# Two VectorE additions of a complex product, placed behind all 18 matmuls instead of behind the first six

## The chip, the cores and the metric

The kernel runs on one core of a Trainium2 chip. The metric is device time in microseconds (us) of one execution. Five engines work side by side, each through its own queue in order: TensorE (PE in the profile; its weight loads are PEld), VectorE (DVE), ScalarE (ACT), GpSimd (POOL) and SyncE (SP). [...] In this kernel SP issues most DMAs and POOL most loads of tables.

## The reference, cut to what matters

The first part of the computation takes a real Fourier transform along the 3072 positions of each of four sequences, multiplies the complex result by a complex 256 x 256 matrix, adds a complex bias, shrinks each part towards zero by 0.01, and transforms back:

```
X  = rfft(x, axis=1)                    # x: 4 x 3072 x 256
Yr = Xr @ w_r - Xi @ w_i + b_r
Yi = Xr @ w_i + Xi @ w_r + b_i
Y  = sign(Y) * max(|Y| - 0.01, 0)       # real and imaginary part apart
y  = irfft(Yr + 1j * Yi)
```

Two feed-forward blocks follow, the first with a gate (width 1024), the second of width 2048. All matrix products of the parts concerned here are made from a high and a low part of each operand: the product of a pair takes three matmuls (high by high, low by high, high by low).

## The kernel before, in words

The transform of length 3072 is split as 96 x 32. For each of the four sequences (called batches here, `b` = 0 to 3) there are three stages: `s1` (L292) transforms over 96 and writes to HBM, `mid` (L327) does the rest of the forward transform, the complex product, the shrinking and the first half of the way back, and `ib` (L442) the last transform, into HBM again. The change lies in `mid`.

`mid` makes 12 rounds, `j` = 0 to 11 (the loop at L407). One round consists of two steps, with a `yield` after each. In the first step come: `ia` (L391), which is the backward transform of an earlier round; the last part of the product before (the shrinking's second half at L379 on VectorE and four small DMAs `yz<-yf` at L382 on SP, which reorder the result); and `s2` (L332), which is eight matmuls, a ScalarE copy `Xh` (L159) and a VectorE subtraction `Xl` (L160) that make the high and the low part. In the second step, batches 1 to 3 first do `split_y` (L386), that is ScalarE's `yh` (L159), which waits for the four DMAs, and VectorE's `yl` (L160); `ia` of the next round's first step reads both. Then comes `mix` (L349).

`mix` makes the complex product with three real products. One PSUM tile `p` of 1024 columns (two banks) holds it: the common product `k1` in columns 512 to 767, that is in the second bank, and the two others in columns 0 to 511, the first bank. On PE it is six matmuls for `k1` and then twelve more (18 more in the first round of a batch). On VectorE there are two additions of `k1` and the bias into `y` (L368), and one addition of columns 0 to 511 to `y` (L375). Then ScalarE computes a `Relu` into `ym` (L377), and VectorE shrinks (L379).

The order of every queue is the order of the Python text, written out by hand (`manual_schedule` at L243): PE, ACT, DVE and POOL keep it. The framework adds the semaphore waits that the reads and writes of tiles call for. PSUM tiles of `s2`, `mix`, `ia`, and of the feed-forward's products share three buffers in turn (`ptile`, L154).

Batch 0 runs its rounds with little beside them but decoding of weights. The steps of batches 1 to 3 are fed one at a time (`feed`, L931) between the blocks of the first feed-forward part: each block is 12 matmuls with 512 columns on PE (`u_k`, L576: tile `pk`; `u_v`, L602: tile `acc`; `u_r`, L563: tile `pr`), with ScalarE and VectorE work for `g`, `gh` and `gl` (L588 to L597). So there is one such block between two steps, in most cases. Whether VectorE's `g` and `gl` stand between the product's additions and its shrinking, or not, depends on which of the two steps comes first in a unit of the feed-forward part; with nine steps to five units this turns over about every fifth round.

Of the kernel before, what the change touches and what calls it, by code (L numbers as in the profile page):

```python
# [107 lines left out]
def fourier_mix_ffn_kernel(  # L108
# [20 lines left out]
    nc = tc.nc  # L129
# [19 lines left out]
    def pad(pool, n):  # L149

        pads.append(n)
        pool.tile([128, n // 4], F32, name=f"pad{len(pads)}")

    def ptile(name):  # L154
        return ps.tile([128, 1024], F32, tag="h", name=name)

    def split(src, h, l):

        nc.scalar.activation(h, src, AF.Copy)  # L159
        nc.vector.tensor_sub(l, src, h.bitcast(F32))  # L160

    def three(o, pairs, first=True, last=True, **kw):

        n = 3 * len(pairs)
        i = 0
        for (lh, ll), (rh, rl) in pairs:
            for a, c in ((lh, rh), (ll, rh), (lh, rl)):
                nc.tensor.matmul(o, a, c, start=first and i == 0, stop=last and i == n - 1, **kw)  # L168
                i += 1
# [73 lines left out]
    with tc.manual_schedule(engines=order):  # L243
# [36 lines left out]
        def take(n):  # L280

            u = head["use"]
            load_chunks(u + n)
            r = [live.pop(u + i) for i in range(n)]
            head["use"] = u + n
            return r

        def fetch(n=AHEAD):

            load_chunks(head["use"] + n)  # L290
# [22 lines left out]
        def load_t(b, j):  # L313

            k = BEHIND[b]
            if j >= NP + k:
                b, j = b + 1, j - NP - k
            if b < B:
                if pad_t:
                    pad(fp, pad_t.pop())  # L320
                t = fp.tile([128, 2, 448], F32R if b else F32, tag="t", bufs=3, name="tt")
                c = slice(0 if j < NP else 192, 192 if j < BEHIND[b] else 448 if b else 320)
                eng = nc.gpsimd if b or j > 2 else nc.scalar
                eng.dma_start(out=t[:, :, c], in_=(tab if b else tab0)[j, :, :, c])
                tt[b, j] = t

        def mid(b):  # L327
            gb = sc_b[b].rearrange("(j g c) n d -> j (c n) g d", g=2, c=4)
            xx, yy = {}, {}
            behind = BEHIND[b]  # L330

            def s2(j):  # L332
                (a,) = take(1)
                t = tt[b, j].bitcast(F32) if b else tt[b, j]
                p = ptile("s2").rearrange("p (dt k g f) -> p dt k g f", dt=2, k=4, g=2)
                for g in range(2):
                    for dt in range(2):
                        w = a[:, g, 128 * dt : 128 * dt + 128]
                        m = 3 if j or g else 2
                        nc.tensor.matmul(p[:, dt, 0:m, g], w, t[:, g, 0 : 64 * m], start=True, stop=True)  # L340
                        if not (j or g):
                            nc.tensor.matmul(p[:, dt, 2:4, g], w, tex, start=True, stop=True)
                xh = fp.tile([128, 2, 448], F32R, tag="Xh", bufs=2, name="Xh")
                xl = fp.tile([128, 2, 448], F32R, tag="Xl", bufs=2, name="Xl")
                w = 384 if j else 448
                split(p.rearrange("p dt k g f -> p dt (k g f)")[:, :, 0:w], xh[:, :, 0:w], xl[:, :, 0:w])
                xx[j] = (xh, xl)

            def mix(j):  # L349
                xh, xl = xx.pop(j)  # L350
                p = ptile("mix")
                k1 = p[:, 512:768]
                part = lambda k, n=128: [
                    ((xh[:, dt, 128 * k : 128 * k + n], xl[:, dt, 128 * k : 128 * k + n]), dt) for dt in range(2)
                ]
                by = lambda w, xs: [(x, (w[0][:, dt], w[1][:, dt])) for x, dt in xs]
                three(k1, by(aw[0], part(2)))
                if pad_y:
                    pad(fp, pad_y.pop())
                y = fp.tile([128, 2, D], F32, tag="y", bufs=2, name="yf")  # L360
                m = fp.tile([128, 2, D], F32, tag="co", bufs=1, name="ym")
                z = fp.tile([128, 2, D], F32, tag="z", bufs=2, name="yz")
                if b:
                    yh = fp.tile([128, 512], F32R, tag="yh", bufs=2, name="yh")
                    yl = fp.tile([128, 512], F32R, tag="yl", bufs=2, name="yl")
                bs = bias[:, 0:2] if j else bias[:, 0::2]
                for a in range(2):
                    nc.vector.tensor_add(y[:, a], k1, bs[:, a])  # L368
                three(p[:, 0:256], by(aw[2], part(1)))
                pi = by(aw[1], part(0))  # L370
                three(p[:, 256:512], pi[:1], last=False)
                if j == 0:
                    three(p[0:64, 256:512], by(aw[0], part(3, 64)), first=False, last=False)
                three(p[:, 256:512], pi[1:], first=False)
                nc.vector.tensor_add(y, y, p[:, 0:512].rearrange("p (a e) -> p a e", a=2))  # L375
                yield
                nc.scalar.activation(m, y, AF.Relu, bias=lam2, scale=-1.0)  # L377
                yield
                nc.vector.scalar_tensor_tensor(y, m, -1.0, y, op0=ALU.mult, op1=ALU.max)  # L379
                for g in range(2):  # L380
                    for a in range(2):
                        nc.sync.dma_start(out=z[64 * a : 64 * a + 64, g], in_=y[64 * g : 64 * g + 64, a])  # L382
                z = z.rearrange("p g e -> p (g e)")
                yy[j] = (z, yh, yl) if b else z

            def split_y(j):  # L386
                if b:
                    y, *yy[j] = yy[j]
                    split(y, *yy[j])

            def ia(j):  # L391
                y = yy.pop(j)
                t = tt.pop((b, j + behind))[:, :, 192:448]
                p = ptile("ia") if b else pa.tile([128, 512], F32, tag="acc", name="ia0")
                for g in range(2):
                    c = slice(256 * g, 256 * g + 256)
                    if not b:
                        nc.tensor.matmul(p[:, c], t[:, g, 0:128], y[:, c], start=True, stop=True)
                        continue
                    yh, yl = y  # L400
                    three(p[:, c], [((t[:, g, 0:128], t[:, g, 128:256]), (yh[:, c], yl[:, c]))])
                sb = fp.tile([128, 2, D], F32, tag="ia", bufs=2, name="iasb")
                nc.scalar.activation(sb.rearrange("p g d -> p (g d)"), p[:, 0:512], AF.Copy)
                nc.sync.dma_start(out=gb[j], in_=sb)

            rest = iter(())
            for j in range(NP + 1):  # L407
                next(rest, None)
                if j < NP:
                    s2(j)  # L410
                if b or j:
                    load_t(b, j + 2)
                if j < NP:
                    yield
                    if j >= 2:
                        split_y(j - 2)
                if j:
                    rest = mix(j - 1)
                    next(rest)
                    fetch(AHEAD if b or j > 6 else 6)  # L420
                    next(rest)
                    yield
                if behind <= j < NP:
                    ia(j - behind)
            next(rest, None)
            split_y(NP - 2)

            def end(j):
                if j == NP - 1:
                    ready.add(("b", b))  # L430
                ia(j)
                if not b and j < NP - 1:
                    load_t(b, j + 6)

            if b:
                ends.extend([lambda: end(NP - 2), lambda: (load_t(b, NP + 3), split_y(NP - 1)), lambda: end(NP - 1)])
            else:
                ends.extend([lambda: end(NP - 3), lambda: end(NP - 2), lambda: end(NP - 1)])
# [670 lines left out]
```

## Time and profile before

| what | value |
|---|---|
| median of 3 runs | 2176.19 us (2174.81 to 2178.41) |
| profiled execution, its time | 2178.48 us |
| profiled execution, its span | 2176.7 us |
| PE busy | 1991.8 us, 92% of the span |
| VectorE busy | 1424.2 us, 65% |
| ScalarE busy | 1243.9 us, 57% |
| mean granted TensorE clock | 0.949 of full |
| rounds of batch 0 | about 40 to 140 us, granted clock 0.87 |
| rounds of batches 1, 2, 3 | about 198 to 372, 452 to 630, 707 to 884 us, granted clock 0.83, 0.84, 0.87 |
| from 1000 us to the end | PE busy 1169.85 of 1177 us, granted clock 1.00 |

The span reaches from the first to the last instruction; 1.8 us of the execution's time lie around it. A row of a timeline or of a list of instructions shows start, duration, engine, line, operation, output and inputs, and, in brackets, how long the engine sat idle before and what ended that. PE rows overlap, since matmuls are pipelined. A row of the chain of waits shows start, duration and what the chain went through there.

### The profile page before, as it was taken

Reading aid. Unit: us, or ns where it says so; the run is one execution under the profiler, and the core shown is the slowest. Engines: PE = TensorE matmul, PEld = TensorE weight load, DVE = VectorE, ACT = ScalarE, POOL = GpSimd, SP = SyncE. Lnnn points to the kernel's source line nnn. Section 1 sums busy time; section 2 is a strip of 40 time slices with the busy share of each in tenths; the row PEclk is TensorE's granted clock in tenths of the full one; section 3 lists DMA queues with packets and bytes.
Section 4 is the critical chain, followed back from the end, with each engine's and each line's share of the span. In section 5 each row is a group of like instructions: output and inputs, shape, how many; then the busy total and the mean of one; then the engine's idle time right before and its main releaser. Section 6 shows DMA issues by size and latency. Waiting matters only on the chain.

```text
span 2176.7 us, 32954 instructions
## 1 busy us (share of the span) xinstructions
PE 1991.8 (92%) x13352; PEld 1817.3 (83%) x13352; DVE 1424.2 (65%) x1813; ACT 1243.9 (57%) x1766; POOL 35.5 (2%) x61
## 2 busy tenths in 40 slices
PE   6679778988789777999999999999999999999998
PEld 3658666777668666888888999999999999999998
DVE  1555444444345544558876887887887887887886
ACT  2345343534245333467775676766766767767765
POOL 0000000000000000000000000000000000000000
PEclk7889788988899988999999999999999999999999
DMA  8476333743257232522221010100100100100100
GB/s 253 144 227 195 87 108 90 222 131 107 73 149 221 82 82 69 154 99 85 84 88 39 20 30 22 36 23 20 35 25 21 32 28 20 31 29 21 31 21 20
DMA packets 121161, 177.18 MB, mean 81 GB/s; under 512 B 16129, under 2 KB 78209, under 8 KB 121009
## 3 DMA queue, kind: packets, MB, share of 16 engines
q1 hardware_dynamic: 110016, 152.91, 23.0%
q0 software_dynamic: 8768, 20.95, 3.8%
q8 instruction: 105, 1.72, 0.3%
q10 hardware_dynamic: 2224, 1.22, 0.2%
q14 instruction: 48, 0.39, 0.1%
HBM read 99.13 MB, written 63.31 MB: 75 GB/s over the span
## 4 chain that ended last, share of the span: by engine, by line
PE 79%; DVE 9%; DMA 4%; ACT 4%; issue 2%; SPq 1%; ACTq 0%; DVEq 0%
PE oacc L857 23%; PE rq L857 14%; PE pk L168 10%; PE acc L168 10%; PE mix L168 6%; PE cc L857 6%; PE ib L453 3%; PE pr L168 2%; DMA yz<-yf 2%; PE s L297 2%; PE s L340 2%; DVE g L596 2%; DVE yf L368 2%; SPq L382 1%; PE pi L168 1%
## 5 line engine op out<-in xcount | busy, mean ns | idle before, releaser
L857 PE MATMUL oacc<-wo_hi,gl 128*128 128x256 f32 x1536 | 424.8, 277 | 1.2 <-DVE gl L798 1.2
L857 PE MATMUL oacc<-wo_hi,gh 128*128 128x256 f32 x1536 | 425.0, 277 | 0.0
L857 PE MATMUL oacc<-wo_lo,gh 128*128 128x256 f32 x1536 | 424.2, 276 | 0.0
L857 PEld LDWEIGHTS oacc<-wo_hi,gl 128*128 128x128 f32 x1536 | 288.7, 188 | 1.8 <-DVE gl L798 1.6
L857 PEld LDWEIGHTS oacc<-wo_hi,gh 128*128 128x128 f32 x1536 | 288.3, 188 | 0.2
L857 PEld LDWEIGHTS oacc<-wo_lo,gh 128*128 128x128 f32 x1536 | 288.3, 188 | 0.0
L789 DVE SCALAR_TENSOR_TENSOR g<-g,c 128x1024 f32<-128x1024 f32 x184 | 225.4, 1225 | 51.8 <-ACT g L785 50.5
L798 DVE TENSOR_TENSOR gl<-g,gh 128x1024 fp32r<-128x1024 f32 x184 | 225.2, 1224 | 40.0 <-ACT gh L795 40.0
L168 PE MATMUL mix<-aw_hi,Xh 128*128 128x256 f32 (+1 forms) x296 | 107.1, 362 | 148.7 <-DVE yf L368 148.7
L785 ACT ACTIVATE g<-c,half 128x1024 f32<-128x1024 f32 x184 | 212.1, 1153 | 5.5 <-DVE c L780 5.2
L857 PE MATMUL rq<-th,sw 128*128 128x256 f32 x1104 | 206.1, 276 | 0.1
L168 PEld LDWEIGHTS mix<-aw_hi,Xh 128*128 128x128 f32 (+1 forms) x296 | 70.5, 238 | 159.8 <-DVE yf L368 158.4
L795 ACT ACTIVATE gh<-g 128x1024 fp32r<-128x1024 f32 x184 | 193.9, 1054 | 1.9 <-DVE g L789 1.9
L775 ACT ACTIVATE s<-rq 128x256 f32<-128x256 f32 x184 | 70.5, 383 | 208.1 <-PE rq L857 208.1
L779 DVE TENSOR_TENSOR c<-rq,s 128x512 f32<-128x512 f32 x184 | 126.6, 688 | 88.9 <-ACT s L775 88.8
L377 ACT ACTIVATE ym<-yf,lam 128x512 f32<-128x512 f32 x48 | 34.7, 723 | 248.4 <-DVE yf L375 248.4
L857 PEld LDWEIGHTS rq<-th,sw 128*128 128x128 f32 x1104 | 166.2, 188 | 0.4 <-ACT s L764 0.3
L588 ACT ACTIVATE g<-pk 128x1024 f32<-128x1024 f32 x96 | 97.9, 1020 | 119.0 <-PE pk L168 118.6
L168 PE MATMUL acc<-gh,wv_hi 128*128 128x512 f32 x384 | 162.9, 424 | 0.0
L168 PE MATMUL pk<-kh,wk_hi 128*128 128x512 f32 x384 | 160.6, 418 | 0.0
L168 PE MATMUL pk<-kh,wk_lo 128*128 128x512 f32 x384 | 154.2, 402 | 0.0
L168 PE MATMUL acc<-gl,wv_hi 128*128 128x512 f32 x384 | 153.8, 400 | 0.0
(152 smaller groups left out, 4728.7 us busy)
## 6 DMA issues: line engine op xcount, KB each, us to landing
yt<-sc_y SPq DMA_DIRECT2D x23, 608.0 KB, 4.3
tt<-in_tab_dram POOLq DMA_DIRECT2D x30, 448.0 KB, 4.3
a<-in_x_dram SPq DMA_DIRECT2D x64, 192.0 KB, 3.9
sc_a<-s1sb SPq DMA_DIRECT2D x32, 384.0 KB, 4.4
a<-sc_a SPq DMA_DIRECT2D x48, 256.0 KB, 3.8
yz<-yf SPq DMA_DIRECT2D x192, 64.0 KB, 2.6
sc_b<-iasb SPq DMA_DIRECT2D x48, 256.0 KB, 4.2
a<-sc_b SPq DMA_DIRECT2D x64, 192.0 KB, 3.2
```

Source lines behind the costliest of these rows:

```text
L168: nc.tensor.matmul(o, a, c, start=first and i == 0, stop=last and i == n - 1, **kw)
L297: nc.tensor.matmul(p[:N1, 512 * i : 512 * i + 512], f1, flat(a), start=True, stop=True)
L340: nc.tensor.matmul(p[:, dt, 0:m, g], w, t[:, g, 0 : 64 * m], start=True, stop=True)
L453: nc.tensor.matmul(p[:, q, et, i], lhs, fi, start=True, stop=True)
L588: nc.scalar.activation(g, p, AF.Relu)
L775: nc.scalar.activation(s[:, 3], q, AF.Copy)
L779: nc.vector.tensor_add(c[:, 1::2], two(rq), s[:, 0:2])
L785: nc.scalar.activation(g, c, AF.Relu, bias=half, scale=1.0 / 6.0)
L789: nc.vector.scalar_tensor_tensor(g, g, 1.0, tmp["c"], op0=ALU.min, op1=ALU.mult)
L795: nc.scalar.activation(h, tmp["g"], AF.Copy)
L798: nc.vector.tensor_sub(hg[i, j][1], tmp["g"], hg[i, j][0].bitcast(F32))
L857: return lambda: nc.tensor.matmul(o, lhs, rhs, start=start, stop=stop, skip_group_check=True)
```

## The change

The two additions at L368 move down, behind the last matmul of the product and directly ahead of the addition at L375. Nothing else is changed: the same instructions, each queue but for its waits in the same order. On VectorE no instruction stood between the additions and that at L375, so its order is the same as well.

```diff
@@ -364,14 +364,14 @@ def mix(j)
                 bs = bias[:, 0:2] if j else bias[:, 0::2]
-                for a in range(2):
-                    nc.vector.tensor_add(y[:, a], k1, bs[:, a])
                 three(p[:, 0:256], by(aw[2], part(1)))
                 pi = by(aw[1], part(0))
                 three(p[:, 256:512], pi[:1], last=False)
                 if j == 0:
                     three(p[0:64, 256:512], by(aw[0], part(3, 64)), first=False, last=False)
                 three(p[:, 256:512], pi[1:], first=False)
+                for a in range(2):
+                    nc.vector.tensor_add(y[:, a], k1, bs[:, a])
                 nc.vector.tensor_add(y, y, p[:, 0:512].rearrange("p (a e) -> p a e", a=2))
                 yield
```

## Rows read from the trace of the kernel before

**Rows 1.** The page: span, and two groups (busy, mean ns; idle before).
```profile
span 2176.7 us, 32954 instructions
...
L168 PE MATMUL mix<-aw_hi,Xh 128*128 128x256 f32 (+1 forms) x296 | 107.1, 362 | 148.7 <-DVE yf L368 148.7
...
L377 ACT ACTIVATE ym<-yf,lam 128x512 f32<-128x512 f32 x48 | 34.7, 723 | 248.4 <-DVE yf L375 248.4
```

**Rows 2.** Waits of PE, whole span: total us, times, longest.
```profile
PE mix L168 <- DVE yf L368: 148.7, 48, 7.8
PE s L297 <- DMA a<-in_x_dram: 8.3, 3, 3.3
...
PE ia L168 <- DVE yl L160: 4.5, 3, 2.7
```

**Rows 3.** Busy time in the four stretches of rounds together (40:140,198:372,452:630,707:884).
```profile
sum 629.00, PE 472.67 PEld 413.22 DVE 307.22 ACT 228.09 POOL 29.89; mean PE 118.17 PEld 103.31 DVE 76.81 ACT 57.02 POOL 7.47
```

**Rows 4.** Waits of PE in the rounds of batch 0 (40 to 140 us).
```profile
PE mix L168 <- DVE yf L368: 26.8, 12, 3.3
```

**Rows 5.** Timeline of PE: the seventh matmul of the first and last product.
```profile
44.49 0.38 PE L168 MATMUL mix<-aw_hi,Xh 128*128 128x256 f32 x1 [1.86 <-DVE yf L368]
...
866.25 0.38 PE L168 MATMUL mix<-aw_hi,Xh 128*128 128x256 f32 x1 [0.85 <-DVE yf L368]
```

**Rows 6.** Chain of waits, 860 to 870 us (start, duration, what).
```profile
863.99 0.71 PE ia L168 x6
...
866.25 1.68 PE mix L168 x12
```

**Rows 7.** Chain of waits, 300 to 330 us: one round.
```profile
309.32 2.95 PE mix L168 x12
...
312.29 0.70 DVE yf L375
...
315.66 1.24 DVE g L596
...
316.92 1.22 DVE gl L597
318.15 0.61 DVE yf L379
...
320.57 3.24 DMA yz<-yf
...
323.92 0.64 ACT yh L159
...
325.27 0.68 DVE yf L368 x2
...
325.99 2.93 PE mix L168 x12
```

**Rows 8.** Chain of waits, 198 to 218 us: another kind of round.
```profile
202.40 3.80 PE mix L168 x18
206.20 2.73 PE acc L168 x12
208.93 1.30 PE s L340 x8
210.23 2.76 PE pk L168 x12
...
213.93 0.63 ACT yh L159
...
215.28 0.68 DVE yf L368 x2
```

**Rows 9.** Timeline of batch 0, 96 to 106 us.
```profile
96.99 0.81 ACT L159 ACTIVATE Xh<-s 128x768 fp32r<-128x768 f32 x1 [1.34 <-PE s L340]
...
98.71 0.75 DVE L368 TENSOR_TENSOR yf<-mix,bias 128x256 f32<-128x256 f32 x2
99.51 0.40 PE L168 MATMUL mix<-aw_hi,Xh 128*128 128x256 f32 x1 [1.85 <-DVE yf L368]
...
105.55 0.80 ACT L159 ACTIVATE Xh<-s 128x768 fp32r<-128x768 f32 x1
```

## The prediction, made before the changed kernel ran

> **What bounds the kernel now.** I read the page first. TensorE is busy for most of the span of 2176.7 us, and the largest idle time that any group of matmuls has ahead of it stands at the product: 148.7 us ahead of `mix`, all put down to VectorE's additions at L368 [rows 1]. The list of PE's waits says the same: 148.7 us in 48 waits, one for each product, the longest 7.8 us, against 8.3 us for the next row [rows 2]. The stretches in which the four batches make their rounds last 629 us together, and PE is busy for 472.67 of them, so it idles 156 us there; the wait at the product is nearly all of that [rows 2, 3]. Of the 148.7 us, 26.8 belong to batch 0 and the other 121.9 to batches 1 to 3 [rows 2, 4].
>
> The timeline then shows where the wait sits: at the seventh matmul, between the six of `k1` and the rest. The first product of the kernel waits 1.86 us there and the last 0.85 us [rows 5]. In batch 0 the seventh matmul starts at 99.51, right when the second addition ends (98.71 + 0.75 = 99.46) [rows 9]; in the chain of waits at 325.99, again 0.04 us after the additions' end [rows 7]. The twelve matmuls write columns 0 to 511 of the tile, the additions read 512 to 767, so the values don't need this order; it comes from both using one tile. PE thus stands still until VectorE has worked off all that is queued ahead of the additions.
>
> **The change part by part.** No instruction is added or removed. PE's 48 waits at the seventh matmul should go, since no VectorE read of the tile is left between the matmuls. Nothing takes their place inside the product.
>
> VectorE's additions now wait for the last matmul instead of the sixth. Queued behind them is the addition at L375, which waited for the last matmul anyway; nothing stands between. So the new wait holds up no other work. It lengthens the way from the last matmul to L375 by the two additions, 0.75 us [rows 9], where VectorE is early. Who waits for that is ScalarE's `ym` and, through it, the four DMAs; PE meets them only one or two blocks later. In the last rounds, where the additions wait for PE, the cover is a block of 2.73 us or more [rows 8]. If that cover were gone everywhere, the cost would be 48 x 0.75 = 36 us.
>
> What is late next? In batches 1 to 3 PE's next dependence on VectorE is `ia`, which reads `yl`, and `yl` stands directly ahead of the additions. After the old stall's place PE still does the twelve matmuls (1.68 us where TensorE had hardly idled [rows 6]) and a block (2.73). So it may now run 4.4 us ahead, plus the 0.75 us of the additions themselves, before it waits again. A stall up to about 5 us does not reappear at once; but rounds follow each other, and then the loop through VectorE, ScalarE and the DMAs sets the pace. I work that loop out for the two kinds of round.
>
> The long round has `g` and `gl` between L375 and the shrinking. From 309.32 to 325.99 it takes 16.67 us [rows 7]: the twelve matmuls until L375 starts at 312.29 (2.97), then L375 0.70, `ym` and two more ScalarE instructions up to 315.66, `g` 1.24, `gl` 1.22, shrinking 0.61 (to 318.76), four DMA issues and a landing until `yh` starts at 323.92 (5.16), `yh` and `yl` until 325.27 (1.35), the additions 0.68. Only the first term goes, because the twelve matmuls are then done before the additions start. New length 13.70, a gain of 2.97. PE's own work in a round at its better speed is 1.68 + 0.84 (half of it, for the six) + 2.73 + 2.76 + 1.30 + 2 x 0.71 = 10.7 us [rows 6, 8], so the loop stays the bound there and PE waits elsewhere, at `ia` or `s2`.
>
> The short round has no `g` in that place. From 202.35 to 215.96 it takes 13.6 us [rows 8], and the chain runs through PE: product, block, `s2`, block, and then `yh`. Its wait is some 2.2 us (216.00 less 212.99 and less 0.84 for six matmuls). Without it the loop is 0.72 for the additions, 0.70, `ym` 0.72 [rows 1], 0.61, 5.16 and 1.35, 9.3 us in all, less than PE's 10.7; so PE bounds it, at 10.7, a gain of 2.9, more than the wait was, since the matmuls behind a wait ran slower (twelve take 2.95 us after a long wait and 1.68 after a short one [rows 6, 7]).
>
> The sum over the 36 products of batches 1 to 3, with each wait and its twelve matmuls read as in [rows 5] (first and last of 48 shown): in 21 the wait is longer than the twelve matmuls, and I count the twelve, 59.2 us. In 9 it is shorter but above 0.85, 19.0 us in all, to which I add 0.6 each (2.9 for 2.3, as above), 24. In 6 it is 0.85, that is the additions alone, 5. This makes 88. For run-ahead that outlasts a long round I add some 5 of the waits not counted: 94. The bounds are 83.3 (the smaller of wait and twelve matmuls, throughout) and 121.9 (all waits).
>
> Batch 0 has no `yh` and `yl`. Its loop is `Xh`, `Xl`, additions, twelve matmuls, L375 and so on to the next `Xh`, from 96.99 to 105.55 in the round shown, 8.56 us [rows 9]. Without the wait PE reaches the next `s2` earlier by it, and the twelve matmuls leave VectorE's loop. The smaller of wait and twelve sums to 21.0 over the 12 products, all waits to 26.8 [rows 4]. I take 18: the stretch behind batch 0 already waits for loads (8.3 us for `x` in three waits [rows 2]), and a shorter batch 0 leaves these less time.
>
> The sum is 94 + 18 = 112 us. The profiled execution took 2178.48 us (its span and 1.8 us around it), so it would take 2066.5; that execution lies 2.3 us above the median shown, and from the median of 2176.19 the same gain leads to 2064.
>
> [...]
>
> **The rivals.**
>
> *All of it comes back.* PE's run-ahead of 5 us carries it through the long rounds, the short rounds catch up, and the low clock goes too. For it: long and short rounds alternate in runs of four or five, and only six of the 48 waits are longer than 5 us (first and last in [rows 5]). Against it: a long round's loop of 13.70 stands 3 us above PE's 10.7, four in a row make 12 us, and that is more than 5. Gain 148.7 and some 5 of clock: about 2022.
>
> *The loop takes it back.* With PE out of the way, the DMA hop of 5.16 us, the in-order queues of ScalarE and VectorE, or PSUM buffers in turn hold the rounds. If the hop and its queue grow by 1 us in each of the 36 rounds, 94 becomes 58; with batch 0 at 15 the gain is 73, and the time 2103. For it: of 16.67 us, only 2.97 were PE's [rows 7]. Against it: VectorE is busy only 307 of 629 us in these stretches and ScalarE 228 [rows 3].
>
> *Slower: the wait is not the tile's.* If what holds the seventh matmul is another thing that ends with VectorE's work there (the split `Xl`, a buffer that comes free), the 48 waits stay, and the additions, now behind the matmuls, lengthen each round's loop by their 0.75 us: 48 x 0.75 = 36 us, 2212. It decides from the first product on. [...] The rows speak against it: the wait ends 0.04 us after the second addition [rows 7, 9], where `Xl` had ended before the first, and by the list all 48 are put down to L368 [rows 2].
>
> *Nothing changes*, because the span is set by transfers: against it stands that PE is the waiting engine and the DMA hop is counted in the loop already.
>
> **How the numbers follow.** The forecast, 2064 with its own range of 2040 to 2090, gets 0.63; all of it, 0.14; the loop takes it back, 0.18; slower, 0.03; no change, 0.02. A change within 0.2% (4.4 us) can't be told from none. The range reaches from 2028, with half of the second case, to 2104, with half of the third. Faster by over 0.2% is 0.63 + 0.14 + 0.18 = 0.95, same 0.02, slower 0.03.
>
> **What would show it.** The list of PE's waits after should have no row for `mix` from L368; in its place rows of 20 to 50 us for `ia` from `yl` or for `s` from L375, in the long rounds. The three stretches of batches 1 to 3 should be some 31 us shorter each, batch 0's 18, and the rest after 1000 us as long as before. VectorE's idle time ahead of L368 should now be ended by `mix` on PE in the short rounds. The twelve matmuls should take 1.7 us in more products than before. I am wrong if PE still waits at the seventh matmul (slower), if the new waits of PE sum to more than 70 us (the loop), or to less than 15 (all of it).

## The result, and the profile after

The changed kernel takes 2030.75 us (median of 4 runs, 2029.24 to 2033.39); the kernel before, run beside it, 2177.30 (4 runs). The ratio is 0.9327, with a 95% interval of 0.931 to 0.9344: 146.5 us faster. The forecast was 2064 with a range of 2028 to 2104. The time lies inside that range, but outside the forecast's own 2040 to 2090; the gain was put at 112 us.

The page of the changed kernel (span; busy time of the engines; granted TensorE clock in 40 slices):

```profile
span 2028.3 us, 32930 instructions
...
PE 1949.9 (96%) x13352; PEld 1776.3 (88%) x13352; DVE 1424.9 (70%) x1813; ACT 1240.8 (61%) x1766; POOL 35.5 (2%) x61
...
PEclk7979999998999899999999999999999999999999
```

The same 13352 matmuls keep PE busy for 41.9 us less than before (1991.8), so this part of the gain is no removed wait: the matmuls themselves ran faster. The rest of the span's 148.4 us, 106.5, is idle time.

PE's waits after, whole span (total us, times, longest), which answer to [rows 2]:

```profile
PE ia L168 <- ACT yh L159: 26.0, 13, 4.2
PE ia L398 <- DMA yz<-yf: 12.3, 9, 2.8
...
PE ia L168 <- DVE yl L160: 7.0, 12, 2.7
...
PE s L297 <- DMA a<-in_x_dram: 5.2, 4, 3.0
...
PE mix L168 <- DVE yf L375: 0.7, 1, 0.7
```

The row of 148.7 us is gone. What is left has moved to `ia`: 26.0 + 12.3 + 7.0 = 45.3 us. Of that, 33.0 (26.0 and 7.0) belong to batches 1 to 3 and 12.3 to batch 0. In the kernel before, `ia` waited for the same three 7.9 us in all (4.5 for `yl`, 2.1 for the DMAs, 1.3 for `yh`).

The next two fences cut both kernels at the same instructions: the first matmul of `s2` of batches 0, 1, 2 and 3, and the last matmul of the last `ib`. Columns: stretch, its length, busy time of the engines, granted clock, DMA share, GB/s. Before:

```profile
36.10:190.30 154.20, 119.86 (x602) 100.33 (x603) 82.18 (x138) 67.69 (x101) 12.73 (x18) 0.86 0.69 213
190.30:446.10 255.80, 212.13 (x1036) 179.10 (x1035) 120.38 (x154) 102.89 (x132) 8.17 (x14) 0.89 0.45 131
446.10:701.50 255.40, 210.66 (x1035) 177.46 (x1034) 119.77 (x153) 104.14 (x133) 8.18 (x14) 0.89 0.44 128
701.50:927.60 226.10, 186.92 (x967) 163.11 (x965) 114.33 (x146) 91.09 (x118) 6.19 (x11) 0.90 0.36 103
```

After:

```profile
37.80:170.10 132.30, 113.30 (x602) 93.39 (x603) 82.71 (x138) 68.11 (x101) 12.66 (x18) 0.88 0.82 248
170.10:379.50 209.40, 197.27 (x1036) 165.27 (x1035) 120.34 (x154) 101.48 (x132) 8.21 (x14) 0.97 0.55 161
379.50:590.40 210.90, 199.32 (x1036) 166.44 (x1035) 119.74 (x153) 103.10 (x133) 8.21 (x14) 0.96 0.53 155
590.40:778.90 188.50, 175.39 (x966) 153.18 (x965) 114.25 (x146) 89.50 (x118) 6.22 (x11) 0.96 0.43 124
```

The four stretches are 21.9, 46.4, 44.5 and 37.6 us shorter, 150.4 in all; ahead of them the changed profile is 1.7 us later, and what follows takes 1249 us in both. In batches 1 to 3 the gain, 128.5 us, is larger than all their waits had been (121.9). PE's idle time in the four stretches falls from 161.9 to 55.8 us (length less busy time), its busy time from 729.6 to 685.3. So 106 us of the gain are idle time and 44 are faster matmuls; in batches 1 to 3 the granted clock rises from 0.89 or 0.90 to 0.96 or 0.97.

### The profile page after: what moved, and what is told of

Read it like the earlier page. It is cut to its first block, busy times and chain, and to the rows that moved or that the text cites. A ratio compares the mean times of both kernels' runs of the same rounds, so it can differ in the third digit from the quotient of the medians.

```text
span 2028.3 us, 32930 instructions
## 1 busy us (share of the span) xinstructions
PE 1949.9 (96%) x13352; PEld 1776.3 (88%) x13352; DVE 1424.9 (70%) x1813; ACT 1240.8 (61%) x1766; POOL 35.5 (2%) x61
## 4 chain that ended last, share of the span: by engine, by line
PE 77%; DVE 8%; DMA 6%; ACT 4%; SPq 3%; issue 1%; ACTq 0%; DVEq 0%
PE oacc L857 25%; PE rq L857 15%; PE acc L168 10%; PE pk L168 9%; PE cc L857 6%; DMA yz<-yf 5%; PE ib L453 3%; PE pr L168 3%; SPq L382 3%; PE s L297 2%; PE s L340 1%; PE mix L168 1%; DVE yf L374 1%; PE pi L168 1%; DVE yf L375 1%
## 5 line engine op out<-in xcount | busy, mean ns | idle before, releaser
L168 PE MATMUL pk<-kh,wk_hi 128*128 128x512 f32 x384 | 155.7, 405 | 0.1
L857 PE MATMUL rq<-tl,sw 128*128 128x256 f32 x552 | 152.5, 276 | 0.7 <-DVE tl L733 0.7
L596 DVE TENSOR_TENSOR g<-g 128x1024 f32<-128x1024 f32 x76 | 93.0, 1223 | 83.8 <-ACT gh L592 83.4
L168 PE MATMUL acc<-gh,wv_lo 128*128 128x512 f32 x384 | 151.8, 395 | 0.0
L168 PE MATMUL pk<-kl,wk_hi 128*128 128x512 f32 x384 | 150.3, 391 | 0.0
```

Of the source, the lines that this page charges most:

```text
L596: nc.vector.tensor_mul(g, g, g)
L857: return lambda: nc.tensor.matmul(o, lhs, rhs, start=start, stop=stop, skip_group_check=True)
```

## The experiments

Theory A, formed on the two traces (48 waits at the seventh matmul before, 148.7 us in all; that row is gone after): PE's next matmul into a PSUM tile is held until VectorE has read the tile, whichever columns either touches, and the length of the wait is what stands in VectorE's queue ahead of that read. The rivals are in the expectations. Each kernel ran beside the kernel before; ratios are to that.

**One column put back.** On the changed kernel:

```diff
                 bs = bias[:, 0:2] if j else bias[:, 0::2]
+                nc.vector.tensor_copy(m[:, 0, 0:1], k1[:, 0:1])
                 three(p[:, 0:256], by(aw[2], part(1)))
```

> The changed kernel with one thing put back: a VectorE copy of a single column of the common product (128 x 1, out of the tile's second bank) stands where the two additions stood, behind the first six matmuls; the additions stay behind all 18. Theory A (any VectorE read of the tile orders PE's next matmul into it behind VectorE's whole queue, so the wait is the queue ahead of the additions and not their own 0.75 us): the 48 waits at the seventh matmul come back, now ended by the copy, some 110 to 125 us in all instead of 148.7 (each shorter by about 0.7), and the time is 2150 to 2185. Rival (the wait was the additions' own work, or belongs to something else that VectorE finishes there): waits of under 20 us, time 2030 to 2045.

Measured: 2172.45 us, ratio 0.9949 (0.9923 to 0.9976). All but some 10 us of the gain are gone. PE's waits in this kernel, and the new copy (min/median/max ns):

```profile
PE mix L168 <- DVE ym L367: 139.4, 48, 7.5
```
```profile
L367 DVE COPY ym<-mix x48: 147/151/159, 42.8 to 858.1; 128x1 f32<-128x1 f32 x48
```

A read of 0.15 us, of column 512, which none of the twelve matmuls writes, brings back 139.4 of 148.7 us. That this column lies in another bank than theirs is my reading of the layout; no run shows where a bank ends. The waits are longer than the 110 to 125 expected; the time is inside theory A's range. So the additions' own work was hardly part of the cost; the queue ahead of them was. The rival that the wait belonged to something else is out, since nothing but a read of the tile was added.

**Half the way.** On the kernel before, the additions go behind the first twelve matmuls:

```diff
-                for a in range(2):
-                    nc.vector.tensor_add(y[:, a], k1, bs[:, a])
                 three(p[:, 0:256], by(aw[2], part(1)))
+                for a in range(2):
+                    nc.vector.tensor_add(y[:, a], k1, bs[:, a])
```

> The kernel before with the two additions moved down half the way: behind the first twelve matmuls (the common product and the first of the two others) and ahead of the last six. Theory A (whole-tile order): the wait moves to the thirteenth matmul and is only as much shorter as six matmuls last (0.7 to 1.4 us): some 100 to 115 us of waits on L368's additions, time 2120 to 2150. Rival B (order goes by bank or columns: columns 0 to 255 were the problem, or having some matmuls queued is enough to cover it): no waits above 20 us, time near 2031.

Measured: 2133.74 us, ratio 0.9777 (0.9755 to 0.9798). PE's waits:

```profile
PE mix L168 <- DVE yf L369: 121.1, 48, 6.6
```

The wait only moves to the thirteenth matmul, somewhat longer than the 100 to 115 expected. Rival B is out. Each wait is 0.6 us shorter on average (27.6 in 48), about the time of the six matmuls that now stand ahead of it (six with 256 columns take 0.71 us [rows 6]).

**Fillers in the waits.** On the kernel before:

```diff
                 three(k1, by(aw[0], part(2)))
+                for _ in range(FILLERS[b][j]):
+                    nc.tensor.matmul(p[:, 768:1024], aw[0][0][:, 0, 0:128], aw[0][0][:, 0], start=True, stop=True)
```

> The kernel before, additions in their old place, with filler matmuls (128 x 256, into the tile's unused columns 768 to 1023) between the sixth and the seventh matmul, as many in each of the 48 products as fit into the wait that its trace shows, less 1.05 us: 833 in all, their results unused. They keep TensorE busy while it waits and take nothing away from the wait. Theory C (a part of the gain is clock: with the waits go low-clock matmuls, 41.9 us of PE busy time between the two profiles): twelve matmuls take about 1.7 us in most products, granted clock above 0.97, and the time is 2120 to 2150, since the twelve stand in the loop. Rival D (the clock is a by-stander; only the waits count): 2165 to 2195, as the loop of VectorE and the DMAs sets the pace anyway.

Measured: 2125.04 us, ratio 0.9743 (0.9719 to 0.9767), at a mean granted clock of 0.990 (before 0.949). PE's waits, and two groups of its matmuls (count, busy us, mean ns, idle before):

```profile
PE mix L174 <- DVE yf L376: 59.1, 48, 2.6
```
```profile
L365 PE MATMUL mix<-aw_hi 128*128 128x256 f32 x833 | 106.2, 283 | 0.0
L174 PE MATMUL mix<-aw_hi,Xh 128*128 128x256 f32 (+1 forms) x296 | 89.9, 304 | 59.1 <-DVE yf L376 59.1
```

No wait was taken away: PE still can't go on before the additions are done, it only does useless work meanwhile. Yet 2.6%, some 56 us, go. A matmul of the group that had taken 362 ns in the mean [rows 1] takes 304. Theory C holds: the idle time had cost clock beyond its own length, and in the kernel before part of this cost lay in the loop of the long rounds, where the twelve matmuls stand [rows 7]. In the 14 long rounds (counted further down) the twelve take 1.74 us in the mean, where they took 2.92, and the round 14.89 instead of 16.61.

**The split behind the Relu, on the kernel before.** `split_y(j - 2)` moves from ahead of `mix(j - 1)` to behind its second part:

```diff
-                    if j >= 2:
-                        split_y(j - 2)
...
                     next(rest)
+                    if 2 <= j < NP:
+                        split_y(j - 2)
```

> The kernel before, additions in their old place, with the split of the reordered result (ScalarE yh, which waits for the four small DMAs, and VectorE yl) moved from ahead of the product to behind ScalarE's Relu of the same round. Theory A: in batches 1 to 3 the waits at the seventh matmul were mostly yl and the DMAs behind it, queued ahead of the additions; they fall from 121.9 to 40 to 60 us (Xl, g and gl are still ahead), batch 0 keeps its 26.8, new waits of some 20 us appear at ia, and the time is 2080 to 2120. Rival E (the wait was Xl, g and gl, not the DMA): waits stay above 95 us, time above 2140.

Measured: 2100.62 us, ratio 0.9624 (0.9605 to 0.9644). PE's waits from 190 to 840 us, which holds the rounds of batches 1 to 3:

```profile
PE mix L168 <- DVE yf L368: 75.5, 36, 5.3
PE ia L168 <- DVE yl L160: 3.9, 3, 2.7
PE ia L168 <- ACT yh L159: 1.7, 2, 1.3
```

Batch 0 keeps 26.4 us. In batches 1 to 3 the waits fall from 121.9 to 75.5, a smaller fall than to the 40 to 60 expected, and no new ones appear at `ia`, against the 20 us expected. So `yl` with its DMAs was 46 us of the waits, and the larger part was the rest of the queue; both theories had seen one part. The time came out inside A's range all the same: 47 us of waits less in the whole kernel (101.8 left) brought 81 us, more than their own length.

**The late additions made twice.** On the changed kernel:

```diff
-                for a in range(2):
+                for a in (0, 1, 0, 1):
                     nc.vector.tensor_add(y[:, a], k1, bs[:, a])
```

> The changed kernel with the pair of late additions made twice over (the second pair writes the same values), so that what stands behind the last matmul on VectorE is 1.5 us instead of 0.75 in each of the 48 products. It prices the wait that the change adds. Theory A (in most rounds TensorE is the bound and the additions hide beside the next block; they count only where VectorE and the four DMAs set the pace, some ten to fifteen rounds): 4 to 14 us slower than the changed kernel, 2034 to 2046. Rival (the additions lie on the path of every round, the price named in the prediction's slower case): 48 x 0.75 = 36 us, some 2067.

Measured: 2057.31 us, ratio 0.9448 (0.9431 to 0.9465); against the changed kernel's 0.9327 this is 26 us dearer. Of the 36 us added to VectorE's queue, three quarters come through. Theory A missed here by a factor of two or more. Where it counts, ScalarE's waits show, in this kernel:

```profile
ACT ym L377 <- DVE yf L375: 156.3, 48, 6.0
```

and in the changed one:

```profile
ACT ym L377 <- DVE yf L375: 125.2, 48, 5.3
```

ScalarE waits for its `Relu` longer by nearly all of the 36 us (31.1), and the DMAs come behind it.

**The late additions left out.** On the changed kernel:

```diff
-                for a in range(2):
-                    nc.vector.tensor_add(y[:, a], k1, bs[:, a])
-                nc.vector.tensor_add(y, y, p[:, 0:512].rearrange("p (a e) -> p a e", a=2))
+                nc.vector.tensor_add(y, bs, p[:, 0:512].rearrange("p (a e) -> p a e", a=2))
```

> The changed kernel without the two late additions: the addition behind the product takes the bias itself and the common product is left out of the result (its six matmuls still run). It prices the additions from the other side. Theory A2, formed on the doubled additions (26 us dearer; in the changed kernel most rounds go at the pace of VectorE's loop and not of TensorE's, so the 0.75 us counts in some three rounds of four): as much is gained as the doubling lost, less what rounds at TensorE's pace of 9.6 us can't give: 2005 to 2016. Rival (doubling hurt because it pushed rounds over an edge, and the changed kernel has them covered): 2024 to 2032.

Measured: 2011.40 us, ratio 0.9232 (0.9214 to 0.9249), 21 us below the changed kernel. By both runs the additions cost some 0.4 to 0.55 us per product in their new place. They don't cost it in the same rounds: leaving them out shortens the 14 long rounds by 0.71 us in the mean and the 19 short ones by 0.24; the second pair lengthens them by 0.58 and 0.62. This is the price of the additions where they now stand. It is not the price of the move, since in the kernel before they stood in the chain as well, with 0.68 us in both kinds of round [rows 7, 8].

**Shortening what is left.** Three edits on the changed kernel, alone and together. `ia` behind `s2`:

```diff
                     s2(j)
+                if b and behind < j <= NP:
+                    ia(j - 1 - behind)
...
-                if behind <= j < NP:
+                if not b and behind <= j < NP:
                     ia(j - behind)
```

> The changed kernel with ia, in batches 1 to 3, moved from ahead of s2 to behind it in the same step: TensorE has eight matmuls (1.3 us) more to do before it needs yl. Theory A (what is left of the wait has moved to ia: 33 us there in batches 1 to 3, in 25 waits): of it some 15 to 20 us fall away, time 2010 to 2020. Rival F (the loop of VectorE and the four DMAs sets those rounds, so a later ia only moves the wait on to s2 or the product): 2026 to 2035, with as much waiting elsewhere.

Two of the four DMAs on another queue:

```diff
-                        nc.sync.dma_start(out=z[64 * a : 64 * a + 64, g], in_=y[64 * g : 64 * g + 64, a])
+                        (nc.gpsimd if b and g else nc.sync).dma_start(out=z[64 * a : 64 * a + 64, g], in_=y[64 * g : 64 * g + 64, a])
```

> The changed kernel with two of the four reordering DMAs of batches 1 to 3 issued by POOL instead of SP. On SP four issues take 2.4 us one after the other ahead of the last one's landing. Theory A (the hop stands in the loop of the long rounds): the hop gets some 1.2 us shorter, waits at ia fall by a third to a half, time 2012 to 2025. Rival G (POOL issues dearer or is held by its table loads, and the hop grows): 2032 to 2050.

The split behind the Relu, the same edit as before, now on the changed kernel:

> The changed kernel with the split of the reordered result (yh, yl) moved behind ScalarE's Relu, as was tried on the kernel before. Additions and their successors no longer queue behind yl and the DMAs. Theory A (in the long rounds the additions wait for yl, so the loop through four DMAs closes each round): that loop opens, but yl, which ia needs, comes later in the round; the waits at ia stay or grow to 30 to 50 us, the time is 2020 to 2040. Rival H (the loop is all that is left): waits of under 15 us in all, time 2000 to 2012.

`ia` behind `s2` with two DMAs on POOL:

> The changed kernel with both: ia behind s2, and two of the four reordering DMAs on POOL. Theory A2 (loop's pace): ia's place gives slack and not pace, POOL gives some 0.6 us in a long round; together not more than a few us beyond either alone (2025 each): 2016 to 2024. Rival (the two gains are independent and add): 2018 to 2020; (they collide: POOL's issues wait behind its table loads, which wait for the later ia): 2028 to 2040.

Two DMAs on POOL with the split behind the Relu:

> The changed kernel with two of the four DMAs on POOL and the split (yh, yl) behind ScalarE's Relu. With the split there, the chain of a round through the DMAs no longer closes at the additions, and rounds of 12.4 us should turn to 10.5; the shorter hop should then pay at ia. Theory A2: 2016 to 2026. Rival (ia's wait for yl takes it all, as with the split alone): 2027 to 2034.

All three:

> The changed kernel with all three: ia behind s2, two DMAs on POOL, split behind Relu. ia's slack is what the late split lacks, so here it should pay: Theory A2: waits at ia under 20 us, time 2005 to 2018. Rival (VectorE's and ScalarE's queues set the pace whatever is reordered): 2020 to 2030.

| on the changed kernel | us | ratio to before, 95% | PE's waits at `ia` in batches 1 to 3, us |
|---|---|---|---|
| (nothing) | 2030.75 | 0.9327 (0.931 to 0.9344) | 33.0 |
| `ia` behind `s2` | 2025.45 | 0.9306 (0.9288 to 0.9325) | 31.5 |
| two DMAs on POOL | 2025.13 | 0.9300 (0.9282 to 0.9318) | 33.1 |
| split behind Relu | 2030.99 | 0.9329 (0.9312 to 0.9346) | 39.4 |
| `ia` and POOL | 2021.76 | 0.9286 (0.9265 to 0.9306) | 30.3 |
| POOL and split | 2028.56 | 0.9320 (0.9302 to 0.9338) | 39.0 |
| all three | 2003.79 | 0.9201 (0.9184 to 0.9217) | 24.5 |

Of the single edits none is clear of the changed kernel's interval; `ia` with POOL is just clear of it, and all three are far from it. With `ia` behind `s2` the waits turn to another cause, as rival F had it; PE's waits in that kernel, from 160 to 730 us:

```profile
PE ia L168 <- DVE yf L375: 16.7, 7, 4.5
PE ia L168 <- ACT yh L159: 8.4, 8, 3.0
PE ia L168 <- DVE yl L160: 6.4, 9, 2.5
```

`ia` now takes the PSUM buffer of a product whose addition at L375 isn't done; the loop has only another place to show. The POOL edit was expected to make the hop 1.2 us shorter and `ia`'s waits shorter by a third to a half; the hop, from the first issue to the last landing, went from 4.52 to 3.90 us in the mean of the 36 products, and the waits stayed. The split alone did what A said, POOL with the split what its rival said, and `ia` with POOL came out in A2's range, where it can't be told from a plain sum of the two. All three together are 27 us faster than the changed kernel, 8% less than the kernel before, and the fastest of all. That is 1 us below A2's range, though the waits at `ia`, 24.5 us, are above the 20 it named. PE's waits there in the same stretch:

```profile
PE ia L168 <- ACT yh L159: 17.3, 11, 4.0
PE ia L168 <- DVE yl L160: 7.2, 13, 2.7
```

The split takes the DMAs out of the loop that closes at the additions, and the later `ia` gives back what the split costs elsewhere. The lengths of the rounds show both, from one addition at L375 to the next (mean of the 14 long and of the 19 short rounds):

| on the changed kernel | long, us | short, us |
|---|---|---|
| (nothing) | 12.65 | 9.45 |
| split behind Relu | 11.07 | 10.74 |
| POOL and split | 11.21 | 10.66 |
| all three | 10.45 | 9.80 |

All three need the split (18 us are lost without it, by `ia` and POOL) and the later `ia` (25 us, by POOL and split). Whether they need POOL is open, as `ia` and split without POOL did not run.

## Why the prediction was right, and where its size was off

**The wait goes, and by the tile's order.** Right. The single column and the half way show it from both sides; the "slower" rival is out.

**New waits at `ia`, 20 to 50 us.** Right in size and place: 33.0 us in batches 1 to 3, and 45.3 with batch 0, between the 15 and the 70 that I had named as signs of being wrong. What ends most of them is `yh` (26.0) and not, as I had said, `yl` (7.0). The other sign, matmuls of `s` held by L375, did not show with the changed kernel; L375 came up with `ia` behind `s2`, at `ia`. The twelve matmuls take 1.6 us, and VectorE's additions wait for PE in ten products, 8.3 us in all, both as forecast.

**The sum for batches 1 to 3: 94 us.** 128.5, and here the size was off. In both traces I measured the 33 rounds that follow another product of their batch, from the start of one addition at L375 to the next. A round is long if `g` and `gl` stand between L375 and the shrinking, and short if not. "Counted" is what my sum had for the same rounds:

| rounds | number | before, mean us | after, mean us | counted, us | gained, us |
|---|---|---|---|---|---|
| long | 14 | 16.61 | 12.65 | 40.9 | 55.3 |
| short, wait longer than its twelve matmuls | 7 | 15.57 | 10.46 | 18.3 | 35.7 |
| short, the others | 12 | 11.65 | 8.86 | 22.1 | 33.5 |

In the second row, where most is missing, a step failed. I had sorted the rounds by their wait and not by their kind: in all 21 whose wait was longer than the twelve matmuls I counted the twelve alone, as if the loop through the DMAs held them. Only 14 are long. In the kernel before, the chain of waits goes through a DMA `yz<-yf` in 13 of these 14 and in none of the other seven. There VectorE's queue ahead of the additions held work of the feed-forward part. The product whose L375 starts at 312.29 [rows 7] is one of the seven; its wait was 4.73 us, and `xf` (L549), which prepares the input of the feed-forward part, stood in that queue. VectorE before, and then after:

```profile
295.16 0.69 DVE L375 TENSOR_TENSOR yf<-yf,mix 128x512 f32<-128x512 f32 x1 [3.02 <-PE mix L168]
...
306.59 1.41 DVE L549 SCALAR_TENSOR_TENSOR xf<-yt,mus,xf 128x512 f32<-128x512 f32 x2
...
312.29 0.69 DVE L375 TENSOR_TENSOR yf<-yf,mix 128x512 f32<-128x512 f32 x1 [3.02 <-PE mix L168]
```
```profile
249.60 0.69 DVE L375 TENSOR_TENSOR yf<-yf,mix 128x512 f32<-128x512 f32 x1
...
257.75 1.41 DVE L549 SCALAR_TENSOR_TENSOR xf<-yt,mus,xf 128x512 f32<-128x512 f32 x2
...
260.45 0.69 DVE L375 TENSOR_TENSOR yf<-yf,mix 128x512 f32<-128x512 f32 x1
```

This round went from 17.13 to 10.85 us, more than its whole wait. In the seven together the waits were 27.7 us and the gain 35.7, where I had counted 18.3. It also follows that long rounds come singly or in pairs, and not in runs of four, as my case against "all of it" had them. In the third row the gain is larger than waits and my 0.6 us together; how much of that is clock and how much is time that PE had lost in the round before, no run here separates.

**The clock.** I had added 0.6 us for faster matmuls to nine waits, 5 us in all; PE's busy time fell by 44. But the two can't be set against each other: 41.6 of the 44 us are the matmuls right behind the former waits (119.5 us before and 77.9 after, over the 48 products), and 26.2 of these stand in the 21 rounds whose twelve matmuls my sum had taken out in whole. So the clock's part of the shortfall can't be read off as 44 less 5, and that my 112 us come near the 106 us of idle time that went is chance. The fillers show that the slow matmuls cost 56 us in the kernel before. They can't show how much of that lay outside my sum. Nor were the matmuls slow behind every wait: in batch 0 of the kernel before, a wait of 2.94 us (at 91.45 us) was followed by twelve matmuls in 1.71, where the wait of 4.73 us at 309.32 was followed by twelve in 2.95 [rows 7].

**The long round: 13.70 us.** 12.50 in the run. The chain of waits of the changed kernel, one long round, from one addition at L375 to the next (start, duration, what), which answers to [rows 7]:

```profile
260.45 0.70 DVE yf L375
261.18 0.72 ACT ym L377
261.90 0.95 ACT kh L557
262.85 0.96 ACT gh L592
263.83 1.24 DVE g L596
265.09 1.22 DVE gl L597
266.31 0.62 DVE yf L379
...
268.74 2.05 DMA yz<-yf
...
270.89 0.64 ACT yh L159
271.55 0.69 DVE yl L160
272.25 0.68 DVE yf L374 x2
...
272.95 0.70 DVE yf L375
```

The twelve matmuls are gone from the chain, as forecast, and term by term it is the old one, but for the last DMA's landing: 2.05 us where [rows 7] has 3.24. In this round that is the whole difference. In the mean of the 14 long rounds the time from the landing to L375 fell from 4.76 to 1.75 us, the 3.0 that I had forecast, and the hop, from the first of the four issues to the last landing, from 4.78 to 4.09, which I had held fixed. Why the DMAs land sooner was not tested.

**The short round: 10.7 us at PE's pace.** The run has 9.6, in this part of the chain of the changed kernel (225.98 to 235.58):

```profile
225.98 2.12 PE mix L168 x18
228.10 2.72 PE pr L168 x12
230.82 0.71 PE ia L168 x6
231.53 1.30 PE s L340 x8
232.82 2.75 PE acc L168 x12
235.58 2.12 PE mix L168 x18
```

I counted `ia` twice: the row of 0.71 us has all six matmuls ([rows 6] say x6), not half of them. And 18 matmuls without a break take 2.12, not 2.52.

**The late additions: no cost from the move.** Open. The prediction put the new wait at nothing, and at 36 us if its cover were gone. Doubling (26 us) and leaving out (21 us) show that the additions are not under cover in their new place: over half of their time is paid. But both my loops, 13.70 and 9.3 us, keep them, as they stood in the chain before the change too [rows 7, 8]. What the move alone adds was not measured.

**Batch 0: 18 us.** 21.9. The sum of the smaller of wait and matmuls had been 21.0, and the waits for `x`, for which I took 3 off, didn't grow (8.3 before, 5.2 after).

**The rivals.** "All of it comes back" has the time nearest (2022) but by luck: it had no waits left and 5 us of clock, where 45 us of waits remain and 44 us of faster matmuls make up for them. "The loop takes it back" is out by size, though its loop is real; the hop that it let grow by 1 us became shorter in the long rounds.

## What to carry to other kernels

Where an engine waits at a tile, ask what order the tile imposes and not only which data are shared: here a read of one column that the matmuls behind it don't write held TensorE 48 times, 139 us in all, because it stood at the end of a long queue. Price a wait on TensorE as idle time plus the slower matmuls around it (here 106 and 44 us), read from the same group at both speeds. Before counting what a round gives back, sort the rounds by the chain that holds them, and not by the length of their wait: a long wait can stand behind a queue that nothing closes into a loop, as seven of 21 did here. And to see what an instruction costs where it stands, double it once and leave it out once.

## What the runs showed of the hardware that wasn't expected

Filling 833 matmuls into the waits, which adds 106.2 us of TensorE work and no result, made the kernel 56 us faster; the mean granted clock rose from 0.949 to 0.990. The prediction had added 5 us for faster matmuls.
